# A check moved to VectorE and a re-ordered first ten microseconds, in a kernel that fills TensorE

## The chip, the cores and the metric

One core of one Trainium2 chip. The metric is the device time of one execution in microseconds; lower is better. The profile gives a "span", from the first to the last recorded work; the time is about 2 us longer than the span. A verdict of faster or slower needs 2%, which is 30 us here.

## The reference, cut to what matters

```python
xn = layernorm(x)                                  # x: 2048 x 1024, bf16
out = x + A(xn, mem0, Wq, Wk, Wv, Wo, 32) + B(xn, w1, w2, w3, w4)

def A(x, mem0, ...):          # 64 segments of 32 tokens, each with 8 memory rows ahead
    mem = mem0
    for s in range(64):
        h = concat(mem, x[32*s:32*s+32])
        o = attention(h) @ Wo                      # 32 heads of 128
        mem = o[:8]; outs.append(o[8:])

def B(x, w1, w2, w3, w4):     # token-mixing MLP
    h = gelu(layernorm(x) @ w1);  x1 = x + shift(h) @ w2
    return x1 + gelu(layernorm(x1) @ w3) @ w4
```

Read literally, A is serial: a segment's memory is the output of the one before. The kernel guesses all 64 memories from segment means, computes everything in parallel, and then checks that the guess agrees with the memories that came out. If it does not, a serial fallback would run. With these inputs it does not run.

## The kernel before: the parts that matter

The order is: normalise x and multiply by w1 (stage 1), w2 (stage 2), w3 and w4 (stage 3, with the guessed memories woven in), then V, attention and output. The start, cut:

```python
load_x(0)                                      # one DMA on the SP queue
for c, q in ((0, nc.scalar), (2, nc.scalar), (1, nc.sync), (3, nc.sync)):
    if q is nc.sync: load_x(1 + c // 2)
    q.dma_start(w1_sb[:, 2*c:2*c+2, :], ...)   # w1 in four chunks of 512 KB
...
def transposes(xn2, xn2T, jj, half, halves=False):
    ps = psum0.tile([P, 4, P], F32, tag="tr")  # one PSUM bank
    for k in range(4):
        nc.tensor.matmul(ps[:, k, :], xn2[...k...], ident[:], start=True, stop=True)
    step = 2 if halves else 4                  # halves: only for tile 0
    for i in range(0, 4, step):
        nc.scalar.copy(xn2T[:, jj, half*4+i : half*4+i+step, :], ps[:, i:i+step])

def stage1_k(xn2T):                            # tile 0: k outermost, so that w1 can trickle in
    for k in range(KT):
        if k == KT - 2: tr(1, 0); tr(1, 1)     # tile 1's transposes
        for co in range(KT): nc.tensor.matmul(pss[co//4][:, co%4, :], w1_sb[:, k, ...], xn2T[:, 0, k, :], ...)
# later tiles: norm on VectorE (up to tile 7) or ScalarE; from tile 6 on transposed by DMA (SP queue)
xn2 = ring.tile([P, D], BF16, tag="xn2")       # 3 buffers
```

The check, cut (the squares are summed over partitions by TensorE):

```python
def row_norms(...):  sq = src * src;  sr = sum over k of sq   # VectorE
    nc.tensor.matmul(ps[:1, :NQ], ones_f[:], sr[:])            # fp32, one row
# in stage 3:  gthr = TOL2 * row_norms(GT)                      ("threshold unit")
# at the end:  okf = row_norms(Dm) <= gthr; another fp32 matmul counts the partitions with bad sums
```

## Time and profile before

| what | value |
|---|---|
| time, first three executions | 1509.73 us median, 1509.59 to 1510.04 |
| span, profiled execution | 1508.1 us |
| TensorE busy | 99% |
| first w1 matmul | 8.04 us |
| w1 matmuls of k 6 and 7, tile 0 | 11.17 us |
| first stage-2 matmul (the chain of waits) | 66.81 us |
| last addition | 1504.35 us |

The line on w1, the first stage-2 matmul and the last addition are anchors: the distance between the same two anchors in two traces tells where time went, to some hundredths of a microsecond, where the times of whole executions scatter by one. Anchors are compared only within one view: where nothing waits, the chain of waits puts a start at the end of the work before it, up to 0.2 us later than the timeline does. The w1 matmuls are given by the timeline, the first stage-2 matmul and the last addition by the chain, unless the text says otherwise. The lines that carry the start and the end are in the prediction.

### The profile page before, as it was taken

Reading aid. Unit: us, or ns where it says so; the run is one execution under the profiler, and the core shown is the slowest. Engines: PE = TensorE matmul, PEld = TensorE weight load, DVE = VectorE, ACT = ScalarE, POOL = GpSimd, SP = SyncE. Lnnn points to the kernel's source line nnn. Section 1 sums busy time; section 2 is a strip of 40 time slices with the busy share of each in tenths; the row PEclk is TensorE's granted clock in tenths of the full one; section 3 lists DMA queues with packets and bytes.
Section 4 is the critical chain, followed back from the end, with each engine's and each line's share of the span. In section 5 each row is a group of like instructions: output and inputs, shape, how many; then the busy total and the mean of one; then the engine's idle time right before and its main releaser. Section 6 shows DMA issues by size and latency. Waiting matters only on the chain.

```text
span 1508.1 us, 24241 instructions
## 1 busy us (share of the span) xinstructions
PE 1498.3 (99%) x9762; PEld 803.5 (53%) x9834; DVE 544.6 (36%) x1136; ACT 501.9 (33%) x1140; POOL 175.6 (12%) x246
## 2 busy tenths in 40 slices
PE   9999999999999999999999999999999999999998
PEld 8744444445444444444456645664665455545555
DVE  8382230100020212221146624651564166516641
ACT  6433103013012011111256614650663266416630
POOL 5241020211111221100000010001000100010001
PEclk9999999999999999999999999999999999999999
DMA  9599762353355787622389956992998299919911
GB/s 313 155 254 329 220 180 88 133 203 113 126 164 147 195 250 253 212 98 84 126 223 254 244 125 175 257 239 68 247 244 203 74 227 228 212 62 200 216 49 51
DMA packets 305380, 272.93 MB, mean 181 GB/s; under 512 B 156023, under 2 KB 272281, under 8 KB 305265
## 3 DMA queue, kind: packets, MB, share of 16 engines
q1 hardware_dynamic: 282800, 189.38, 50.5%
q0 software_dynamic: 21776, 80.85, 15.6%
q8 instruction: 79, 1.29, 0.4%
q10 hardware_dynamic: 688, 1.11, 0.2%
q14 instruction: 37, 0.30, 0.1%
HBM read 190.08 MB, written 45.29 MB: 156 GB/s over the span
## 4 chain that ended last, share of the span: by engine, by line
PE 97%; DVE 1%; DMA 1%; issue 0%; POOL 0%; ACT 0%; SPq 0%; POOLq 0%
PE ps L667 30%; PE pso L725 15%; PE ps L601 15%; PE ps L542 13%; PE ps L568 13%; PE ps L400 4%; PE ps L318 2%; PE psS L682 2%; PE psO L706 2%; PE ps L865 1%; PE ps L492 1%; PE gps L471 0%; PE ps L457 0%; DMA wt<-in_A_Wq_dram 0%; DVE st L262 0%
## 5 line engine op out<-in xcount | busy, mean ns | idle before, releaser
L667 PE MATMUL ps<-hTb,wt 128*128 128x396 bf16 (+2 forms) x2528 | 485.0, 342 | 0.1
L667 PEld LDWEIGHTS <-wt 128*128 128x128 bf16 x2528 | 236.7, 98 | 175.8 <-DMA wt<-in_A_Wq_dram 0.5
L601 PE MATMUL ps<-wt,xT 128*128 128x512 bf16 x1003 | 220.1, 379 | 1.1
L725 PE MATMUL pso<-wo_sb,oX 128*128 128x512 bf16 (+1 forms) x972 | 208.5, 372 | 1.1
L542 PE MATMUL ps<-xn3T,w_sb 128*128 128x512 bf16 x896 | 196.2, 379 | 0.0
L568 PE MATMUL ps<-w_sb,h3T 128*128 128x512 bf16 x873 | 194.3, 379 | 1.2
L601 PEld LDWEIGHTS <-xT 128*128 128x128 bf16 x1024 | 100.2, 98 | 120.8
L543 ACT ACTIVATE h3T<-ps 128x512 bf16<-128x512 f32 x112 | 66.8, 597 | 290.4 <-PE ps L542 289.5
L725 PEld LDWEIGHTS <-oX 128*128 128x128 bf16 x992 | 96.3, 98 | 107.4
L669 ACT CAST KT<-ps 128x462 bf16<-128x462 f32 (+2 forms) x160 | 81.7, 510 | 203.0 <-PE ps L667 198.8
L568 PEld LDWEIGHTS <-h3T 128*128 128x128 bf16 x896 | 87.0, 98 | 103.4
L542 PEld LDWEIGHTS <-w_sb 128*128 128x128 bf16 x896 | 86.6, 98 | 102.0
L688 DVE TENSOR_REDUCE sums<-sm 99x4 f32<-99x396 f32 (+2 forms) x176 | 97.6, 555 | 114.9 <-ACT sm L686 114.9
L671 ACT ACTIVATE QT<-ps 128x462 bf16<-128x462 f32 (+2 forms) x160 | 83.8, 524 | 120.6 <-PE ps L667 106.6
L603 ACT CAST Vs<-ps 128x512 bf16<-128x512 f32 x64 | 37.5, 585 | 233.2 <-PE ps L601 174.9
L684 DVE TENSOR_TENSOR sm<-psS,c_mask_reg_sb 99x396 f32<-99x396 f32 x152 | 86.7, 570 | 71.7 <-PE psS L682 71.4
L607 DVE CAST Vs<-ps 128x512 bf16<-128x512 f32 x64 | 44.3, 692 | 171.6 <-PE ps L601 163.2
L686 ACT ACTIVATE sm<-sm 99x396 f32<-99x396 f32 (+2 forms) x176 | 92.8, 527 | 35.0 <-DVE sm L684 28.2
L694 DVE TENSOR_TENSOR Pn<-sm,rs 99x396 bf16<-99x396 f32 (+2 forms) x176 | 98.9, 562 | 7.1 <-DMA PT<-Pn 0.8
L732 POOL DMA_DIRECT2D out_dram<-ot x30 | 16.4, 546 | 698.9 <-DVE ot L731 693.0
L569 DVE TENSOR_TENSOR R<-ps,R 128x512 f32<-128x512 f32 x32 | 21.9, 689 | 175.3 <-PE ps L568 154.9
L731 DVE TENSOR_TENSOR ot<-pso,Rt 128x512 bf16<-128x512 f32 (+1 forms) x33 | 22.3, 675 | 170.4 <-PE pso L725 166.2
(123 smaller groups left out, 1048.3 us busy)
## 6 DMA issues: line engine op xcount, KB each, us to landing
wt<-in_A_Wq_dram SPq DMA_DIRECT2D x76, 512.0 KB
wt<-in_A_Wk_dram SPq DMA_DIRECT2D x76, 512.0 KB
wt<-in_A_Wv_dram POOLq DMA_DIRECT2D x24, 1024.0 KB, 6.5
V_scratch<-Vs SPq DMA_DIRECT2D x32, 512.0 KB
V<-V_scratch SPq DMA_DIRECT2D x40, 384.0 KB
R_scratch<-x POOLq DMA_DIRECT2D x16, 512.0 KB, 4.7
R<-R_scratch SPq DMA_DIRECT2D x16, 512.0 KB
R_scratch<-R POOLq DMA_DIRECT2D x16, 512.0 KB, 3.8
```

The lines of the kernel that those rows point to most:

```text
L542: nc.tensor.matmul(ps[:].rearrange("p (n t) -> p n t", t=P), w3_sb[:, k, f * P:(f + 1) * P], xn3T[tb][:, :, k, :], start=(k == 0), stop=(k ...
L543: nc.scalar.activation(h3T[:, f, :], ps[:], ACTF.Gelu_apprx_tanh)
L568: nc.tensor.matmul(ps[:], h3T[:, f, j * P:(j + 1) * P], w4_sb[:, f, ch * 512:(ch + 1) * 512], start=(f == 0), stop=(f == FT - 1))
L601: nc.tensor.matmul(ps[:], xT[:, m4 * 4 + j, k, :], wv[:, k, :], start=(k == 0), stop=(k == KT - 1))
L667: nc.tensor.matmul(ps[:, :nb], w[:, k, hh * P:(hh + 1) * P], B["hT"][:, k, :nb], start=(k == 0), stop=(k == KT - 1))
L669: nc.scalar.copy(dst[:, hh, :], ps[:, :nb])
L671: nc.scalar.mul(dst[:, hh, :], ps[:, :nb], scale)
L684: nc.vector.tensor_tensor(sm[:T, :, :T], S3, t["mask"][:].unsqueeze(1).to_broadcast((T, 4, T)), op=ALU.add)
L686: nc.scalar.activation(e[:T, :, :T], sm[:T, :, :T], ACTF.Exp, scale=LN2)
L688: nc.vector.tensor_reduce(ss, e[:T, :, :T], axis=AX.X, op=ALU.add)
L694: nc.vector.tensor_tensor(Pn[:T, :, :T], e[:T, :, :T], rs[:T, :].unsqueeze(2).to_broadcast((T, 4, T)), op=ALU.mult)
L725: nc.tensor.matmul(self.ps[:, :self.w], self.oX[0][:, h, self.oX[1] + self.gl * P:self.oX[1] + (self.gl + 1) * P], wo_sb[:, h, self.cc], s ...
```

## The change

Its intent: let tile 0 land and be copied sooner, take the identity and the memory out of later places, and take the check's small matmuls from TensorE. The core of the diff:

```diff
-    ident = const_tile("c_ident", np.eye(P))          # by DMA
+    ident = cpool.tile([P, P], BF16)                  # memset on VectorE, affine_select on POOL
+    mask40 = const_tile("c_mask40", _serial_mask())   # for the fallback, loaded with the constants
@@ load_x
+    if n == 0:
+        nc.scalar.dma_start(xts[n][:, 512:], x_v[:, n, 512:])
+        nc.sync.dma_start(xts[n][:, :512], x_v[:, n, :512])
@@ norm_stats                                          # tile 0: the needed column of the power first
-    nc.gpsimd.tensor_tensor(rr[:], ab[:], neghalf[:], op=ALU.pow)
+    for c in (slice(1, 2), slice(0, 1)) if n == 0 else (slice(0, 2),):
+        nc.gpsimd.tensor_tensor(rr[:, c], ab[:, c], neghalf[:, c], op=ALU.pow)
@@ transposes
-    for k in range(4):
-        nc.tensor.matmul(ps[:, k, :], ...)
     step = 2 if halves else 4
     for i in range(0, 4, step):
+        for k in range(i, i + step):
+            nc.tensor.matmul(ps[:, k, :], ...)
         nc.scalar.copy(..., ps[:, i:i + step])
@@ after tile 0's transposes                           # was in stage 3
+    for k in range(KT):
+        nc.tensor.matmul(ps9[:, k, :], m0[...], eye9[:], start=True, stop=True)
     load_consts(4)
+    nc.gpsimd.memset(sums[:], 1.0)                     # was before everything else
@@ stage 3: threshold unit removed;  norm1(5) one step later
@@ end: row sums, 32x32 transposes and reductions, all on VectorE; no matmul
@@ fallback (not taken): three whole weight loads per segment instead of 24 partial ones
```

More of the change, by code (lines that the diff above doesn't have):

```diff
@@ L130, in load_consts @@
             nc.gpsimd.dma_start(t[:], d.ap())
-    ident = const_tile("c_ident", np.eye(P, dtype=np.float32))
-    load_consts(1)
-    eye9 = const_tile("c_eye9", np.concatenate([np.eye(M, dtype=np.float32), np.ones((M, 1), np.float32)], 1))
+    ident = cpool.tile([P, P], BF16)
+    nc.vector.memset(ident[:], 1.0)
+    eye9 = cpool.tile([M, M + 1], BF16)
+    c0 = cpool.tile([P, KT, 1], F32)
     mask_first = const_tile("c_mask_first", _tile_mask(3, True))
@@ L137 @@
     mask_two = const_tile("c_mask_two", _tile_mask(2, False))
+    mask40 = const_tile("c_mask40", _serial_mask())
     GT = cpool.tile([P, KT, NQ], F32)
     MZ = cpool.tile([P, KT, NQ + 1], BF16)
-    gthr = cpool.tile([1, NQ], F32)
     flag_i = cpool.tile([1, 1], I32)
@@ L151, with row_sums @@
     sums = cpool.tile([P, NTILE * 8, 4], F32)
-    nc.gpsimd.memset(sums[:], 1.0)
     SH = (-1, -1, 1, 1, -2, -2, 2, 2)
-    def row_norms(pool, ppool, tag, src, in_place=False):
-        sq = src if in_place else pool.tile([P, KT, NQ], F32, tag="nsq", bufs=1)
-        nc.vector.tensor_tensor(sq[:], src[:], src[:], op=ALU.mult)
-        sr = pool.tile([P, NQ], F32, tag="nsr", bufs=1)
-        nc.vector.tensor_reduce(sr[:], sq[:].rearrange("p k r -> p r k"), axis=AX.X, op=ALU.add)
-        ps = ppool.tile([P, 512], F32, tag=tag)
-        nc.tensor.matmul(ps[:1, :NQ], ones_f[:], sr[:], start=True, stop=True)
-        return ps
+    def row_sums(src):
+        nc.vector.tensor_tensor(src[:], src[:], src[:], op=ALU.mult)
+        sr = smp.tile([P, NQ], F32, tag="nsr")
+        nc.vector.tensor_reduce(sr[:], src[:].rearrange("p k r -> p r k"), axis=AX.X, op=ALU.add)
+        return sr
     SEGS = ((3,) * 4,) * 3 + ((3,) * 4 + (2,), (2,) + (3,) * 4)
@@ L233, in load_x @@
                             xts[n] = ring.tile([P, D], BF16, tag="xt", bufs=10, name=f"xt{n}")
-                            nc.sync.dma_start(xts[n][:], x_v[:, n, :])
+                            if n == 0:
+                                nc.scalar.dma_start(xts[n][:, 512:], x_v[:, n, 512:])
+                                nc.sync.dma_start(xts[n][:, :512], x_v[:, n, :512])
+                            else:
+                                (nc.gpsimd if n == 12 else nc.sync).dma_start(xts[n][:], x_v[:, n, :])
+                    m0 = hTB[:M, 0, 16:16 + D]
+                    nc.gpsimd.dma_start(m0, A_mem0[0])
+                    nc.gpsimd.affine_select(ident[:], ident[:], [[-1, P]], ALU.is_equal, 0.0, base=0, channel_multiplier=1)
+                    nc.gpsimd.memset(eye9[:, M:M + 1], 1.0)
+                    nc.gpsimd.tensor_copy(eye9[:, 0:M], ident[:M, :M])
                     load_x(0)
@@ L293, in transposes @@
                         ps = psum0.tile([P, 4, P], F32, tag="tr")
-                        for k in range(4):
-                            nc.tensor.matmul(ps[:, k, :], xn2[:, (half * 4 + k) * P:(half * 4 + k + 1) * P], ident[:], start=True, stop=True)
                         step = 2 if halves else 4
                         for i in range(0, 4, step):
+                            for k in range(i, i + step):
+                                nc.tensor.matmul(ps[:, k, :], xn2[:, (half * 4 + k) * P:(half * 4 + k + 1) * P], ident[:], start=True, stop=True)
                             nc.scalar.copy(xn2T[:, jj, half * 4 + i:half * 4 + i + step, :], ps[:, i:i + step])
@@ L349 @@
                     tr(0, 1, True)
+                    ps9 = psum.tile([P, KT, M + 1], F32, tag="mm", bufs=4, name="ps9")
+                    for k in range(KT):
+                        nc.tensor.matmul(ps9[:, k, :], m0[:, k * P:(k + 1) * P], eye9[:], start=True, stop=True)
                     norm_stats(1)
+                    nc.vector.tensor_copy(MZ[:, :, 0:M], ps9[:, :, 0:M])
+                    nc.vector.tensor_copy(c0[:], ps9[:, :, M:M + 1])
                     nc.gpsimd.memset(hTB[:, :, 0:2], 0.0)
@@ L369, in ahead @@
                         norm_stats(n + 1, 1)
-                        norm1(n - 2)
+                        if n == 6:
+                            norm1(n - 2)
                     stage1(3, 1, tiles2[2], {0: [lambda: tr(4, 0)], 2: [lambda: tr(4, 1), lambda: ahead(6)], 4: [lambda: tr(5, 0)], 5: [lambda: tr(5, 1), lambda: ahead(7)]}, 1)
@@ L378, in prep @@
                         norm_stats(n + 1)
+                        if n == 8:
+                            norm1(n - 3)
                         norm1(n - 2)
@@ L435, in seg_sums @@
                         nc.vector.tensor_reduce(xb[:, :, 4 * n:4 * n + 4], xr[:].rearrange("p k (s t) -> p k s t", t=SEG), axis=AX.X, op=ALU.add)
-                m0 = ring.tile([M, D], BF16, tag="nsq", bufs=1)
-                nc.gpsimd.dma_start(m0[:], A_mem0[0])
+                    if n == 0:
+                        nc.vector.tensor_tensor(xb[:, :, 0:1], c0[:], xb[:, :, 0:1], op=ALU.add)
                 for c in range(7):
                     nc.sync.dma_start(w4_sb[:, 4 * c:4 * (c + 1), :], w4_v[:, 4 * c:4 * (c + 1), :])
-                def mem_start():
-                    ps9 = psum3.tile([P, KT, M + 1], F32, tag="vr")
-                    for k in range(KT):
-                        nc.tensor.matmul(ps9[:, k, :], m0[:, k * P:(k + 1) * P], eye9[:], start=True, stop=True)
-                    nc.vector.tensor_copy(MZ[:, :, 0:M], ps9[:, :, 0:M])
-                    nc.vector.tensor_tensor(xb[:, :, 0:1], ps9[:, :, M:M + 1], xb[:, :, 0:1], op=ALU.add)
                 def unit_vb(hg):
@@ L478, in unit_g @@
                     return run
-                def unit_thr():
-                    ps = row_norms(ring, psum3, "vr", GT)
-                    nc.vector.tensor_scalar(gthr[:], ps[:1, :NQ], TOL2, None, op0=ALU.mult)
                 def unit_vr(hg):
@@ L510, in spec_load @@
                         pending.append(u(i))
-                        if u is unit_g and i == 7:
-                            pending.append(unit_thr)
                 def spec_step(depth=1):
@@ L572 @@
                                 spec_step(depth)
-                        elif n == 3:
-                            mem_start()
                         elif n > 3:
@@ L873 @@
         nc.vector.tensor_scalar(inr[:, 1:2], lo[:, 1:2], SUM_HIGH, None, op0=ALU.is_le)
-        bad = smp.tile([P, 1], F32, tag="bad", bufs=1)
-        nc.vector.tensor_tensor(bad[:], inr[:, 0:1], inr[:, 1:2], op=ALU.mult)
-        nc.vector.tensor_scalar(bad[:], bad[:], -1.0, 1.0, op0=ALU.mult, op1=ALU.add)
-        for o in rest[:2]:
+        dsum, gsum = row_sums(Dm), row_sums(GT)
+        col = smp.tile([P, 96], F32, tag="col", bufs=1)
+        nc.vector.memset(col[:], 0.0)
+        nc.vector.scalar_tensor_tensor(col[:, :NQ], gsum[:], TOL2, dsum[:], op0=ALU.mult, op1=ALU.subtract)
@@ new lines @@
+        nc.vector.tensor_tensor(col[:, NQ - 1:NQ], inr[:, 0:1], inr[:, 1:2], op=ALU.mult)
+        nc.vector.tensor_scalar(col[:, NQ - 1:NQ], col[:, NQ - 1:NQ], -1.0, None, op0=ALU.add)
+        colT = smp.tile([P, 3, 32], F32, tag="colT", bufs=1)
+        nc.vector.transpose(colT[:].rearrange("p c r -> p (c r)"), col[:])
+        part = smp.tile([P, 3], F32, tag="part", bufs=1)
+        nc.vector.tensor_reduce(part[:], colT[:], axis=AX.X, op=ALU.add)
+        four = smp.tile([32, 4, 3], F32, tag="four", bufs=1)
@@ new lines @@
+        for q in range(4):
+            nc.vector.tensor_copy(four[:, q, :], part[32 * q:32 * q + 32, :])
+        okf = smp.tile([32, 3], F32, tag="okf", bufs=1)
+        nc.vector.tensor_reduce(okf[:], four[:].rearrange("p q c -> p c q"), axis=AX.X, op=ALU.add)
+        nc.vector.tensor_scalar(okf[:], okf[:], 0.0, None, op0=ALU.is_ge)
+        sqr = smp.tile([32, 32], F32, tag="sqr", bufs=1)
+        nc.vector.memset(sqr[:], 1.0)
+        nc.vector.tensor_reduce(sqr[:, 0:1], okf[:], axis=AX.X, op=ALU.min)
@@ L878 @@
+        sqrT = smp.tile([32, 32], F32, tag="sqrT", bufs=1)
+        nc.vector.transpose(sqrT[:], sqr[:])
+        alike = smp.tile([1, 1], F32, tag="alike", bufs=1)
+        nc.vector.tensor_reduce(alike[:], sqrT[0:1, :], axis=AX.X, op=ALU.min)
+        nc.vector.tensor_scalar(alike[:], alike[:], -1.0, 1.0, op0=ALU.mult, op1=ALU.add)
+        nc.vector.tensor_copy(flag_i[:], alike[:])
+        for o in rest:
             for p in range(8):
                 o.piece(p)
-        psd = row_norms(iop, apsum, "S", Dm, in_place=True)
@@ L881 @@
-        okf = smp.tile([1, NQ], F32, tag="okf", bufs=1)
-        nc.vector.tensor_tensor(okf[:], psd[:1, :NQ], gthr[:], op=ALU.is_le)
-        nok = smp.tile([1, 1], F32, tag="nok", bufs=1)
-        nc.vector.tensor_reduce(nok[:], okf[:, 0:NQ - 1], axis=AX.X, op=ALU.add)
-        psc = apsum.tile([P, 512], F32, tag="O", bufs=2)
-        nc.tensor.matmul(psc[:1, :1], bad[:], ones_f[:], start=True, stop=True)
-        cnt = smp.tile([1, 1], F32, tag="cnt", bufs=1)
-        nc.vector.tensor_scalar(cnt[:], nok[:], -1.0, float(NQ - 1), op0=ALU.mult, op1=ALU.add)
@@ L889 @@
-        nc.vector.tensor_tensor(cnt[:], psc[:1, :1], cnt[:], op=ALU.add)
-        nc.vector.tensor_copy(flag_i[:], cnt[:])
-        for o in rest[2:]:
-            for p in range(8):
-                o.piece(p)
-    cond = nc.values_load(flag_i[0:1, 0:1], min_val=0, max_val=NQ + P)
+    cond = nc.values_load(flag_i[0:1, 0:1], min_val=0, max_val=1)
     with tc.If(cond > 0):
@@ L899 @@
             fbig = fctx.enter_context(tc.tile_pool(name="fbig", bufs=1))
-            fw = fctx.enter_context(tc.tile_pool(name="fw", bufs=4))
+            fw = fctx.enter_context(tc.tile_pool(name="fw", bufs=1))
             fr = fctx.enter_context(tc.tile_pool(name="fr", bufs=2))
@@ L903 @@
             nc.sync.dma_start(wo_sb[:], Wo_v)
-            mask40_d = nc.inline_tensor(_bf(np.tile(_serial_mask(), (1, 8))), name="c_mask40")
-            mask40 = fbig.tile([L, 8 * L], BF16)
-            nc.sync.dma_start(mask40[:], mask40_d.ap())
             hseg = fbig.tile([P, KT, L], BF16)
@@ L922 @@
                 nc.vector.tensor_copy(hseg[:, :, M:L], psx[:])
-                for hg in range(8):
-                    cs_ = slice(hg * 512, (hg + 1) * 512)
-                    hs_ = slice(hg * 4, (hg + 1) * 4)
-                    wq = fw.tile([P, KT, 512], BF16, tag="w")
-                    nc.sync.dma_start(wq[:], Wq_v[:, :, cs_])
-                    wk = fw.tile([P, KT, 512], BF16, tag="w")
-                    nc.sync.dma_start(wk[:], Wk_v[:, :, cs_])
-                    wv = fw.tile([P, KT, 512], BF16, tag="w")
-                    nc.sync.dma_start(wv[:], Wv_v[:, :, cs_])
-                    ps = fps.tile([P, 4, L], F32, tag="mm")
-                    for hh in range(4):
-                        for k in range(KT):
-                            nc.tensor.matmul(ps[:, hh, :], wq[:, k, hh * P:(hh + 1) * P], hseg[:, k, :], start=(k == 0), stop=(k == KT - 1))
-                    nc.scalar.mul(QTa[:, hs_, :], ps[:], QSCALE)
-                    ps = fps.tile([P, 4, L], F32, tag="mm")
-                    for hh in range(4):
-                        for k in range(KT):
-                            nc.tensor.matmul(ps[:, hh, :], wk[:, k, hh * P:(hh + 1) * P], hseg[:, k, :], start=(k == 0), stop=(k == KT - 1))
-                    nc.scalar.copy(KTa[:, hs_, :], ps[:])
-                    ps = fps.tile([P, 512], F32, tag="mm")
-                    for k in range(KT):
-                        nc.tensor.matmul(ps[:L, :], hseg[:, k, :], wv[:, k, :], start=(k == 0), stop=(k == KT - 1))
-                    nc.vector.tensor_copy(Va[:, cs_], ps[:L, :])
@@ new lines @@
+                for which, src in enumerate((Wq_v, Wk_v, Wv_v)):
+                    w = fw.tile([P, KT, H * DH], BF16, tag="w")
+                    nc.sync.dma_start(w[:], src)
+                    for hg in range(8):
+                        hs_ = slice(hg * 4, (hg + 1) * 4)
+                        if which < 2:
+                            ps = fps.tile([P, 4, L], F32, tag="mm")
+                            for hh in range(4):
+                                h = hg * 4 + hh
+                                for k in range(KT):
+                                    nc.tensor.matmul(ps[:, hh, :], w[:, k, h * P:(h + 1) * P], hseg[:, k, :], start=(k == 0), stop=(k == KT - 1))
+                            if which == 0:
+                                nc.scalar.mul(QTa[:, hs_, :], ps[:], QSCALE)
+                            else:
+                                nc.scalar.copy(KTa[:, hs_, :], ps[:])
+                        else:
+                            cs_ = slice(hg * 512, (hg + 1) * 512)
+                            ps = fps.tile([P, 512], F32, tag="mm")
+                            for k in range(KT):
+                                nc.tensor.matmul(ps[:L, :], hseg[:, k, :], w[:, k, cs_], start=(k == 0), stop=(k == KT - 1))
+                            nc.vector.tensor_copy(Va[:, cs_], ps[:L, :])
@@ L946 @@
                 for g8 in range(4):
                     psS = fps.tile([L, 8, L], F32, tag="S", bufs=1)
-                    nc.tensor.matmul(psS[:].rearrange("p h k -> p (h k)"), ident[:L, :L], mask40[:], start=True, stop=False, skip_group_check=True)
+                    nc.tensor.matmul(psS[:], ident[:L, :L], mask40[:].unsqueeze(1).to_broadcast((L, 8, L)), start=True, stop=False, skip_group_check=True)
                     for hh in range(8):
```

## The prediction

> **What bounds the kernel now.** I read the page's busy shares first, then the chain of waits, then the timeline of the first 40 us and of the last 70 us, because the diff touches the two ends. Share of the span by engine, then the chain that ended last, by engine and by line:
>
> ```profile
> PE 1498.3 (99%) x9762; PEld 803.5 (53%) x9834; DVE 544.6 (36%) x1136; ACT 501.9 (33%) x1140; POOL 175.6 (12%) x246
> ...
> PE 97%; DVE 1%; DMA 1%; issue 0%; POOL 0%; ACT 0%; SPq 0%; POOLq 0%
> ```
>
> TensorE is the chain for 97% of 1508.1 us. So work taken from DVE, ACT, POOL or a queue is worth nothing, except where TensorE waits for it: in the chain, that is only before 31.73 us and after 1504.35 us. In between, a change pays only by what it takes out of TensorE's own stream. The start, in the chain in order of time (start us, duration us, what):
>
> ```profile
> 0.76 3.30 DMA xt<-in_A_x_dram
> 4.08 0.69 DVE st L259
> 4.78 0.60 DVE st L262
> 5.40 0.22 DVE mv L263
> 5.65 0.23 DVE ab L264
> 5.96 0.73 POOL rr L265
> 6.72 0.73 DVE xn L274 x2
> ```
>
> The reader is to see a serial path: the first x tile lands at 4.06 us, VectorE takes statistics, POOL raises to a power, VectorE normalises, and only then can TensorE transpose. The timeline of the same stretch shows TensorE (start, duration; the bracket is idle time and its releaser):
>
> ```profile
> 1.38 5.30 PE L335 MATMUL warm<-wz 128*128 128x512 bf16 x12 [1.38 <-DVE wz L329]
> 7.19 0.72 PE L295 MATMUL ps<-c_ident_sb,xn 128*128 128x128 bf16 x8 [0.51 <-DVE xn L274]
> 7.62 1.20 ACT L298 CAST xn2T<-ps 128x256 bf16<-128x256 f32 x4 [4.36 <-PE ps L295]
> 8.04 2.84 PE L308 MATMUL ps<-xn2T,w_sb 128*128 128x128 bf16 x48
> 12.29 0.72 POOL L265 TENSOR_TENSOR rr<-ab,neghalf 128x2 f32<-128x2 f32 x1
> 14.29 0.39 PE L295 MATMUL ps<-c_ident_sb,xn 128*128 128x128 bf16 x4
> ```
>
> Useful work starts at 7.19 us, and twelve warm-up matmuls keep TensorE occupied until 6.68 us: between them lie only 0.51 us. The end, by the chain:
>
> ```profile
> 1487.31 2.75 PE pso L725 x12
> 1490.07 0.21 PE ps L163 x2
> 1490.28 0.03 PE psc L886 x2
> 1490.31 14.01 PE pso L725 x96
> 1504.32 0.02 issue
> 1504.35 0.42 DVE ot L731
> ```
>
> The old check's two small float matmuls (L163, L886) interrupt the last output product for 0.24 us; nothing else of the check is on the chain. The last addition and the last store (from 1504.35 to 1508.1) stay as they are.
>
> **What the Trainium skill says.** (1) "DMA: Bandwidth & Descriptors", section "Issuing engines are not separate DMA queues": transfers issued by different engines run on the same 16 DMA engines and interleave; issuing from two only saves sequencer time. The trace agrees that the engines are shared: from 1.38 to 7.19 us the DMA share is 0.93 at 319 GB/s, and from 7.19 to 15 us 1.05 to 1.07 at 385 to 393 GB/s. So halves on two queues help only by changing what else is ahead of the tile. (2) "TensorE: Matmul & The Clock Gate", Part 1: the array runs at half clock until a window of about 3.4 us of activity has passed, the window being free-running. The trace agrees in kind: the warm-up matmuls are 0.43 us apart, the full-clock ones of the same width later 0.22 us (10.74 us for 49). (3) "GPSIMD Engine Reference", section 3.1, says the cost on POOL is a dispatch term plus a term per element. The trace has the power at 558 ns median for 128x1 (L408) and 702 to 942 ns for 128x2 (L265), so one column instead of two saves about 0.15 us, not half.
>
> **The change part by part.** *First x tile in halves.* Before, the tile's 0.25 MB (SP queue) share the engines with the first w1 chunk (ACT queue). Shared evenly, 0.5 MB at 385 GB/s take 1.3 us. With a half on each queue, both ahead of w1, 0.25 MB take 0.65 us. Estimate from those rates: landing at 3.4 us instead of 4.06, 0.65 us gained. The w1 chunks come later by one half tile on the ACT queue (0.13 MB, 0.3 us) and earlier on SP; by the same sum the last chunk lands near 9.9 us and is wanted near 10.4.
>
> *Power of the needed column first:* 0.15 us. *Copies after two transposes instead of four:* two matmul starts of 0.06 us, 0.12 us. Together the start path would be 0.65 + 0.15 = 0.8 us shorter: the first transposes could start at 6.4 us. But the warm-up block holds TensorE until 6.68 us, 6.75 with one more VectorE memset ahead of it. So they start near 6.8 us: 0.4 us gained, not 0.8.
>
> *Identity on chip:* replaces a 32 KB transfer that took 5.5 us to land (issue at 1.22 us, so 6.7 us), which did not hold 7.19 but would hold a start before 6.7. A VectorE memset and three POOL operations (under 1 us each by POOL's 0.71 us memset of 128x704) are done by about 4 us, before POOL's first power. *Memory first:* eight tiny matmuls move here from 218.76 us, where the chain has them at 0.28 us. Here they stand between tile 0's transposes and the first w1 matmuls; the transposes take 0.5 us when not waiting (6.8 to 7.3), the eight end near 7.6, and the first ACT copy (before: 7.62 to 7.92) would be done near 7.4. So w1 matmuls start near 7.6 instead of 8.04: net gain still 0.4. The memory's own load (16 KB, issued near 1.2 us) needs to land by 7.3; the small constants took 4.9 to 6.3 us.
>
> *POOL order:* the 0.71 us memset of sums goes behind the four constant loads, ahead of tile 2's power. That would move it from 12.29 to at best 12.2 us; tile 2 is then normalised by 13.6 and its transposes are wanted at 14.29 - 0.4 = 13.9. Close, but no wait. After this the VectorE chain is almost where it was, so the rest rests on TensorE being fed. *norm1 moved out of the tile-7 step:* 0.54 us of VectorE work leaves the chain that ends in POOL's nm at 29.37, ACT's xn at 29.67 and the stall of 0.25 us at 31.69. ACT can start 0.6 us sooner, TensorE wants it 0.4 us sooner: the stall goes. Start in all: 0.4 + 0.25 = 0.65 us (between 0.1 and 0.9).
>
> *Memory matmuls out of the MLP:* -0.28 us. *Threshold matmul out* (L163 at 427.47): -0.21 us. *Check to VectorE:* -0.24 us of TensorE. On VectorE it adds two squares (0.75 us each, one of them new), two reductions (1.17 us each, one new), and some sixteen small ones of 0.15 to 0.3 us: about 7 us from 1476.8 on, so done near 1484. VectorE has 3.06 us of work in 1476.1 to 1490, so there is room; an output addition due at 1483.2 may slip by a microsecond, and TensorE has other accumulators to go on with. The flag is ready 20 us before it is read. *Fallback:* not taken, so its transfers and loops cost nothing.
>
> Sum: 0.65 + 0.28 + 0.21 + 0.24 = 1.4 us. 1509.73 - 1.4 = **1508.3 us**, 0.1% less.
>
> **The rivals.** *A new wait at the start takes the gain:* the memory's load or the last w1 chunk lands late, or the moved memset makes tile 2 late. For it: DMA is at its full 385 GB/s there and the two margins are 0.3 to 0.5 us. Against it: tiny loads landed in 4.9 to 6.3 us. It would give 1508.7 to 1509.6. *The array is still at half clock when the transposes start earlier:* the window is free-running, the twelfth warm-up matmul is still slow; up to 0.3 us back. *The whole 0.8 us come through* if some warm-up matmuls run at full clock and end early: 1507.7. *The check on VectorE becomes the end:* only if it delayed the last addition at 1504.35, 20 us after it should be done; I give this under 3%. It would cost 1 to 5 us.
>
> **Range and chances.** The three middle and end terms (0.73 us) are read straight off the chain and are safe. The start may give from 0 to 1.2 us. Runs of the kernel before spread over 0.45 us. That makes 1507.0 to 1509.5. A change of 2% is 30 us; nothing in the diff is of that size, in either direction.
>
> **What would show it.** Right: statistics of tile 0 start at 3.4 to 3.5 us; first transposes at 6.7 to 6.9; the w1 matmuls near 7.6; no TensorE idle at 31.7; first stage-2 matmul near 66.0 instead of 66.81; neither small float matmul in the chain at 427 and 1490; the last addition 1.4 us earlier, and 3.7 us from it to the end as before. Wrong: a TensorE wait on the memory's load or a w1 chunk before 11 us, one on tile 2's norm near 14 us, or output accumulators waiting for VectorE after 1477 us.

## More of the kernel before

One more, from the timeline of TensorE (start us, duration us, engine, line, operation), turned out to matter:

```profile
11.17 1.06 PE L308 MATMUL ps<-xn2T,w_sb 128*128 128x128 bf16 x16
```

These are tile 0's matmuls with the last w1 chunk. No wait stands in the brackets, so nothing shows how close to waiting they are. No bracket is not the same as room to spare.

## The result and the profile after

| | before | after |
|---|---|---|
| median of six executions, same rounds | 1510.35 us | 1509.99 us |
| range | 1509.59 to 1511.12 | 1509.44 to 1511.17 |
| profiled span | 1508.1 us | 1508.9 us |
| first w1 matmul | 8.04 us | 8.82 us |
| w1 matmuls of k 6 and 7 | 11.17 us | 13.28 us |
| first stage-2 matmul | 66.81 us | 68.77 us |
| last addition | 1504.35 us | 1505.54 us |

The ratio is 0.9999, with an interval of 0.9986 to 1.0012. The predicted 1508.3 us and the whole range up to 1509.5 lie below the measured median. Part of that distance is the starting point: six executions of the kernel before spread over 1.53 us, where the first three had spread over 0.45, and their median is 0.62 us above the 1509.73 that the forecast started from. Of the gain of 1.4 us that was forecast, the medians show 0.36, which is inside the noise.

The page of the changed kernel still has TensorE as the bound:

```profile
PE 98%; DMA 1%; issue 0%; DVE 0%; SPq 0%; ACT 0%; POOL 0%
```

The chain of waits at the start (start us, duration us, what):

```profile
3.51 0.69 DVE st L265
...
6.46 0.30 PE ps L304 x2
...
6.78 0.38 ACT xn2T L305
...
7.21 0.29 PE ps L304 x2
...
7.51 0.66 ACT xn2T L305 x2
...
8.21 0.37 PE ps L304 x2
...
8.88 4.11 PE ps L315 x48
...
68.77 0.22 PE ps L416
```

The reader is to see three things. The first tile is there sooner, as forecast: statistics at 3.51 us instead of 4.08, the power in 0.58 us instead of 0.73, transposes at 6.46 instead of 7.19. Then the chain alternates between TensorE and ScalarE, twice: transposes, a copy, transposes, copies. Before, the four transposes of a half ran together. And the 48 w1 matmuls are slow: 4.18 us in the timeline, where they had taken 2.84 before (the chain, above, has 4.11). The granted clock explains the last point (columns: stretch, length, TensorE busy and its instructions, granted clock, DMA share, GB/s):

```profile
4.85:8.26 3.41, 1.74 (x12) 1.00 1.02 365
...
9.82:10.32 0.50, 0.50 (x8) 0.50 1.06 393
12.32:12.82 0.50, 0.50 (x13) 1.00 1.02 377
```

From 8.3 to 11.6 us the clock is at half. In the 3.41 us ahead of the fall, TensorE was busy for 1.74 us, 51%. The two costs add up, all by the timelines: 0.78 us later at the first w1 matmul, and 1.34 us longer from there to the transposes that follow the 48 (12.84 - 8.82 against 10.72 - 8.04). Less the 0.16 us that a stall near 31.7 us cost the trace before (from k 6 and 7 to stage 2 it took 55.48 us, the changed kernel 55.32), that is 1.96 us, which is 68.77 - 66.81.

The end, by the chain, and VectorE's part of it in the timeline:

```profile
1488.85 16.66 PE pso L726 x108
...
1505.54 0.42 DVE ot L732
```

```profile
1478.32 0.75 DVE L158 TENSOR_TENSOR Dm<-Dm 128x568 f32<-128x568 f32 x1
...
1485.05 0.14 DVE L899 CAST flag_i<-alike 1x1 int32<-1x1 f32 x1
```

No small matmul interrupts the output product any more. The check takes VectorE from 1478.3 to 1485.2 us; TensorE never waits for it. From the first stage-2 matmul to the last addition the kernel before takes 1437.54 us (1504.35 - 66.81), the changed one 1436.77: 0.77 us gained. So in these two traces the start lost 1.96 us and the rest won 0.77; the tail after the last addition, 3.75 us before and 3.36 after, makes up the span's +0.8 us.

**Theory.** Half of a transposed tile lies in one PSUM tile (PSUM: the memory that the kernel's matmuls write to) of one bank; with copies after each pair, the second pair's transposes must wait until ScalarE has read the first. The waits cost time, and in some executions they empty TensorE enough that its clock falls. **Rivals:** the moved memory matmuls or the halved tile cost the time; the clock falls by itself; the slow matmuls wait for w1.

### The profile page after: what moved, and what is told of

It reads as the page before. It is cut to its first block, busy times and chain, and to the rows that moved or that the text cites. A ratio compares the mean times of both kernels' runs of the same rounds, so it can differ in the third digit from the quotient of the medians. Undisturbed runs are those within 1.5% of the kernel's fastest.

```text
span 1508.9 us, 24248 instructions
## 1 busy us (share of the span) xinstructions
PE 1498.3 (99%) x9757; PEld 804.7 (53%) x9828; DVE 546.8 (36%) x1148; ACT 502.3 (33%) x1140; POOL 175.5 (12%) x250
## 4 chain that ended last, share of the span: by engine, by line
PE 98%; DMA 1%; issue 0%; DVE 0%; SPq 0%; ACT 0%; POOL 0%
PE ps L668 30%; PE ps L602 15%; PE pso L726 15%; PE ps L545 13%; PE ps L571 13%; PE ps L416 4%; PE ps L325 3%; PE psS L683 2%; PE psO L707 2%; PE ps L866 1%; PE ps L497 1%; PE gps L480 0%; PE ps L466 0%; DMA wt<-in_A_Wq_dram 0%; PE ps L315 0%
## 5 line engine op out<-in xcount | busy, mean ns | idle before, releaser
L546 ACT ACTIVATE h3T<-ps 128x512 bf16<-128x512 f32 x112 | 66.8, 597 | 290.8 <-PE ps L545 289.8
```

The costliest lines, as they stand in the source:

```text
L546: nc.scalar.activation(h3T[:, f, :], ps[:], ACTF.Gelu_apprx_tanh)
```

## The experiments

Twelve runs were made, in three jobs (e5 and e6 are the two kernels once more); within a job they share one chip and the runs of the kernel before. All gave correct results. e6 was one look, all others five executions.

| run | median us | before, same job | span of its trace | first stage-2 matmul | executions with mean clock under 1.0 |
|---|---|---|---|---|---|
| e1 four, then copies | 1509.11 | 1509.79 | 1511.6 | 67.88 | 0 of 5 |
| e2 before + interleaving | 1511.83 | 1509.79 | 1510.6 | 68.97 | 4 of 5 |
| e3 own PSUM tiles | 1509.21 | 1509.79 | 1506.9 | 67.17 | 0 of 5 |
| e4 filled gaps | 1509.37 | 1509.79 | 1507.6 | 67.95 | 0 of 5 |
| e5 after again | 1510.25 | 1509.63 | 1508.0 | 69.05 | 3 of 5 |
| e6 before again | 1509.72 | 1509.63 | 1507.9 | 66.56 | 0 of 1 |
| e7 old fallback | 1510.26 | 1509.63 | 1507.8 | 67.57 | 3 of 5 |
| e8 more buffers | 1508.64 | 1509.63 | 1506.9 | 67.21 | 0 of 5 |
| e9 middle and end only | 1509.95 | 1510.26 | 1507.2 | 66.67 | 0 of 5 |
| e10 starts mended | 1509.25 | 1510.26 | 1507.0 | 66.57 | 0 of 5 |
| e11 mask in fallback | 1509.86 | 1510.26 | 1508.1 | 68.24 | 2 of 5 |
| e12 whole first tile | 1509.76 | 1510.26 | 1508.0 | 68.50 | 0 of 5 |

No ratio is clear of noise (each interval is about 0.0013 either side and holds 1). So the verdicts below rest on anchors in the traces and on counts of executions, not on medians.

### e1: the interleaving undone

```diff
-    for i in range(0, 4, step):
-        for k in range(i, i + step): nc.tensor.matmul(ps[:, k, :], ...)
+    for k in range(4): nc.tensor.matmul(ps[:, k, :], ...)
+    for i in range(0, 4, step):
         nc.scalar.copy(...)
```

> The changed kernel with one part undone: four transposes of a half, then the two copies, as before. Theory (the copy of the first pair makes the next pair's transposes wait, because both pairs lie in one PSUM tile; those waits empty TensorE and, in some executions, let its clock fall to half): the first w1 matmul starts near 7.7 us instead of 8.82, its 48 matmuls take 2.7 us, the first stage-2 matmul starts near 66.1 us, time near 1508.2 us. Rival 1 (the memory matmuls or the halved tile cost the time): w1 still starts at 8.5 us or later. Rival 2 (the clock falls by itself, whatever the waits): 48 w1 matmuls at 4 us in about half of the executions here too.

```profile
7.51 3.08 PE L315 MATMUL ps<-xn2T,w_sb 128*128 128x128 bf16 x48
...
11.07 1.07 PE L315 MATMUL ps<-xn2T,w_sb 128*128 128x128 bf16 x16
```

The waits are gone and the first w1 matmul is at 7.51 us, near the expected 7.7. But the matmuls of k 6 and 7 start at 11.07 us: 0.1 us ahead of the 11.17 of the kernel before, although TensorE had begun half a microsecond sooner. Weight loads waited for w1 chunks, 0.23 us ahead of 8.62 and 0.21 us ahead of 11.07. Then a second thing took time: the first stage-2 matmul was expected at 66.1 us and came at 67.88. ScalarE's timeline, then TensorE's waits (total us, times, longest):

```profile
29.99 1.24 ACT L283 ACTIVATE xn<-xt,nm,rr 128x1024 bf16<-128x1024 bf16 x1 [1.42 <-DMA xn2T<-xn]
...
37.61 1.24 ACT L283 ACTIVATE xn<-xt,nm,rr 128x1024 bf16<-128x1024 bf16 x1 [1.12 <-DMA xn2T<-xn]
```

```profile
PE ps L545 <- DMA w_sb<-in_B_w_dram: 3.5, 3, 1.7
...
PE ps L325 <- ACT hTB L327: 1.1, 1, 1.1
```

ScalarE, ready to normalise tiles 8 and 11, waits 1.42 and 1.12 us for transposing transfers, and TensorE then waits 1.1 us for ScalarE. This trace is also the slowest execution of all (span 1511.6 us against 1506.2 to 1507.3 in the other four): 3.5 us of it are a wait for a late weight chunk at the start of stage 3, which no other trace has. It is a miss of the forecast time and no part of the cause.

### e2: the interleaving alone, in the kernel before

The same diff as in the change, `transposes` only.

> The kernel before with that one part alone: two transposes, copy, two transposes, copy for tile 0. Theory: two waits of about 0.5 us each appear before the second pair of each half, the first w1 matmul starts near 9.0 us instead of 8.04, and the time is 1.0 us longer (2.3 us where the clock falls as well): 1511.0 to 1512.5 us. Rival (the interleaving is harmless, the memory matmuls make the delay): w1 starts near 8.0 us, time unchanged.

```profile
7.76 0.38 PE L297 MATMUL ps<-c_ident_sb,xn 128*128 128x128 bf16 x4 [0.46 <-ACT xn2T L298]
8.76 0.37 PE L297 MATMUL ps<-c_ident_sb,xn 128*128 128x128 bf16 x2 [0.62 <-ACT xn2T L298]
8.93 4.27 PE L308 MATMUL ps<-xn2T,w_sb 128*128 128x128 bf16 x48
```

The two waits appear, 0.46 and 0.62 us, as in the changed kernel, without its halved tile and without its memory matmuls. The w1 matmuls take 4.27 us at a clock of 0.50. All five executions lie above all nine of the kernel before in this job (1511.23 to 1512.59 against 1509.17 to 1510.65). The first rival falls: the interleaving is enough to bring the waits and the slow matmuls. (In the medians of this job it costs 2.04 us; the interval of the ratio, 0.9997 to 1.0025, still holds 1.)

### e3: interleaved, but each pair in a PSUM tile of its own

```diff
     for i in range(0, 4, step):
+        if i: ps = psum0.tile([P, 4, P], F32, tag="trh")
         for k in range(i, i + step): ...
```

> The changed kernel with the interleaving kept, but each pair of transposes in a PSUM tile of its own. Theory (the wait is for the shared tile, not for TensorE, the weights or the norm): the waits of transposes on the copy vanish, first w1 matmul near 7.6 us, first stage-2 matmul near 66.0 us, time 1508.1 us, at most 0.2 us from the run with four transposes then copy. Rival (the pairs wait for something else, as the norm of the second half): w1 still near 8.8 us.

```profile
6.41 0.72 PE L306 MATMUL ps<-ident,xn 128*128 128x128 bf16 x8 [0.81 <-DVE xn L281]
...
7.34 1.07 PE L317 MATMUL ps<-xn2T,w_sb 128*128 128x128 bf16 x16
8.78 1.96 PE L317 MATMUL ps<-xn2T,w_sb 128*128 128x128 bf16 x32 [0.37 <-DMA w_sb<-in_B_w_dram]
...
11.24 1.07 PE L317 MATMUL ps<-xn2T,w_sb 128*128 128x128 bf16 x16
```

No transposes wait for a copy; w1 starts at 7.34 us. So the wait was for the shared tile. (The new tile also lies in another bank; two tiles in one bank were not run, so tile and bank are not told apart.) The Trainium skill states the ground for it: "PSUM — Partial Sum Buffer", section "PSUM bank collisions raise a hardware error", says that two engines must not be in one bank and quadrant at once, reads and writes alike, and advises guarding by bank and not by address. No run here lets two engines meet in a bank. The traces show a program that keeps them apart: the pairs wrote disjoint columns, and in one bank they waited 0.46 and 0.62 us, in two banks not at all. The reader also sees the next limit: 0.37 us for a w1 chunk at 8.78, and 11.24 for k 6 and 7. Stage 2 came at 67.17 us, not near the expected 66.0.

### e4: the two waits filled with idle matmuls

```diff
+        for _ in range(3 if i else 0):
+            nc.tensor.matmul(warm[:, :256], wz[:, :P], wz[:, :256], start=True, stop=True)
```

> The changed kernel with three idle 256-column matmuls on zeros ahead of the second pair of each half, which fill most of the two waits; nothing else. Theory of two costs (waits and clock): the waits stay, w1 starts at 8.8 to 9.1 us, but the granted clock stays full and the 48 w1 matmuls take 2.7 us in all executions; first stage-2 matmul near 67.3 us; time near 1509.4 us with no executions near 1511. Rival (the slow w1 matmuls have another cause, as late weights): 48 matmuls still take 4.1 us.

```profile
8.30 0.27 PE L306 MATMUL ps<-ident,xn 128*128 128x128 bf16 x2 [0.29 <-ACT xn2T L307]
...
8.79 2.85 PE L317 MATMUL ps<-xn2T,w_sb 128*128 128x128 bf16 x48
```

The work still waits for the copies and w1 starts at 8.79 us, as in the changed kernel, but 48 matmuls take 2.85 us, and none of the five executions shows a lowered mean clock. The third rival falls: nothing was changed for w1, and the slow matmuls of the changed kernel stand in a stretch whose granted clock is 0.50.

The second rival asks why the clock falls in some executions only. The clock records in the traces tell more than the counts (ahead of the first record the column above shows 1.00, so here the first record itself is used). Full clock was granted at 4.81 us in the changed kernel's trace, as late as 7.39 in others. Where it came early, the last warm-up matmuls ran 0.22 us apart instead of 0.43, and the block ended sooner. It took 5.30 us in the kernel before, whose grant came at 6.77 us, and here 4.39:

```profile
1.48 4.39 PE L342 MATMUL warm<-wz 128*128 128x512 bf16 x12 [1.48 <-DVE wz L336]
```

In the two traces with a fall, the clock fell 3.41 us after it had been granted. How busy TensorE was in these first 3.41 us:

| trace | full clock from | TensorE busy in the next 3.41 us | clock after that |
|---|---|---|---|
| changed kernel | 4.81 us | 1.74 us, 51% | half |
| e2 | 5.10 | 1.53, 45% | half |
| e3 | 4.27 | 2.60, 76% | full |
| e12 | 4.53 | 2.35, 69% | full |
| e4 | 5.00 | 2.40, 70% | full |
| e5 | 6.98 | 2.33, 68% | full |
| e7 | 7.27 | 2.60, 76% | full |

So an early grant alone does not bring the fall (e3, e4, e12), nor do the waits alone (e5, e7): it fell where the two came together and left TensorE half empty. The other seven traces are at about 80% or more, and none falls. One trace each is little, but e4's five executions and the 30 of e1, e3, e8, e9, e10 and e12 without a lowered mean clock agree with it.

### e5 and e6: both kernels once more

No edit.

> The changed kernel itself once more, for more executions and a second trace. Theory (two costs at the start: waits of 1.1 us in every execution, a clock that falls to half in some): executions fall in two groups, spans near 1507.6 us with a mean clock of 1.0 and near 1508.7 with 0.999; in a trace without the fall the 48 w1 matmuls take 2.7 us and the first stage-2 matmul starts near 67.4 to 67.9 us. Rival (the fall is in every execution): all spans near 1508.8.

> The kernel before once more, for a second trace of it. Theory (its gap of 0.51 us ahead of the first transposes lets the clock fall in some executions too): span near 1507.6 us without the fall, near 1508.5 with it, and in the second case the w1 matmuls take over 3.5 us for 48. Rival: the clock never falls in the kernel before.

e5's trace has no fall: 48 matmuls in 2.85 us from 8.95 us on, and k 6 and 7 at 12.09. But TensorE then lost 1.32 us on the way to stage 2, which came at 69.05 us and not at 67.4 to 67.9, for this reason:

```profile
40.94 1.25 PE L325 MATMUL ps<-xn2T,w_sb 128*128 128x256 bf16 x10 [1.32 <-DMA xn2T<-xn]
```

A transposing transfer needed 7.47 us to land, and TensorE waited for it. Of the eleven executions of the changed kernel, five have a mean clock below 1.0, with spans of 1508.1 to 1508.9 us and one of 1512.1; the six others lie between 1507.3 and 1508.1. The groups are there, less far apart than expected; what made the one of 1512.1 so long is not known. e6 shows the kernel before at full clock: stage 2 at 66.56 us, not a wait between 8 and 66 us. Its executions scatter too (spans 1507.2 to 1509.1 in the three jobs), yet only 2 of 27 show a lowered mean clock (so it does fall there at times, as the theory had it). What makes that scatter is not settled.

### e7 and e11: the untaken fallback, and its mask

e7 puts the whole fallback of the kernel before back into the changed one; e11 only moves the load of the 40x40 mask back into it.

> The changed kernel with the untaken fallback of the kernel before put back, and nothing else. The time is longer than the profiled span by 1.96 us in the kernel before and by 2.24 in the changed one. Theory (the shape of the untaken branch sets that difference): it goes back to 1.96 us, the span stays, the time is 0.28 us shorter than that of the changed kernel, near 1509.7. Rival (it is the start or the check): the difference stays 2.24.

> The changed kernel, with only the fallback's mask loaded inside the fallback again instead of with the constants; its seven transfers and loops stay the changed ones. If the shape of the untaken loops makes time minus span 0.33 us longer, it stays near 2.2 us; if the mask's place does, it falls to 1.84 us as in the kernel before.

The time is longer than the span by 2.24 us in the changed kernel (mean of six; 2.17 in e5), by 1.84, 1.97 and 1.98 in the kernel before in the three jobs. In e7 it is 1.79, in e11 1.77. So a part of 0.2 to 0.4 us belongs to this program, and moving the mask alone removes it, with the changed loops left in. But e12, with the mask still among the constants and the first tile in one transfer, has 1.94, and e1, with two halves, 2.21. e8, with the mask outside as well, has 2.04, and e3, which it builds on, 2.32. So edits that have nothing to do with the mask move it too, and what it is stays open. Nor do the medians show a gain: 1510.26 in e7, 1510.25 for the changed kernel in the same job (e5). It lies outside anything that the trace shows.

### e8: buffers for ScalarE, on top of e3

```diff
-    xn2 = ring.tile([P, D], BF16, tag="xn2")
+    xn2 = xn_keep[3][:, n - 8] if 8 <= n < 12 else ring.tile([P, D], BF16, tag="xn2")
```

> The changed kernel with own PSUM tiles (as in e3) and, besides, four other buffers for the normalised tiles 8 to 11, in memory that lies idle then. Theory (when TensorE is early, ScalarE waits for the transposing transfers of tiles 6 to 9 to give their buffers back, TensorE then waits for ScalarE): the ScalarE waits on these transfers (1.8 us in e3, 2.5 in e1) go, TensorE has no idle time between 24 and 42 us, first stage-2 matmul near 66.4 to 66.8 us, span near 1506.3. Rival (the transfers' landing itself is needed by TensorE): the idle time stays, now as a wait for the transposed tile.

```profile
PE ps L317 <- DMA w_sb<-in_B_w_dram: 0.4, 1, 0.4
PE ps L327 <- DMA xn2T<-xn: 0.4, 1, 0.4
```

ScalarE no longer waits for transfers (none in its list), so buffers were what held it. TensorE still waits 0.4 us, now for the transposed tile itself: the rival is right as well, and stage 2 came at 67.21 us, not at 66.4 to 66.8. Its chain from tile 2 to tile 7 runs over VectorE without a gap and begins behind POOL's constants and the moved memset, which put tile 2's power at 12.07 us.

### e9: the middle and the end alone, in the kernel before

Only the check on VectorE and the missing threshold unit.

> The kernel before with only the check on VectorE and the threshold unit out; its start, its memory matmuls and its fallback as before. Theory (the middle and end terms of the sum are real, 0.43 us at the threshold and 0.35 us at the check between anchors of the two traces): first stage-2 matmul as before (66.5 to 66.9 us), TensorE from the first stage-3 matmul to the last addition 0.6 to 0.8 us shorter, span near 1507.0 us in executions at full clock, time near 1508.9, time minus span as before. Rival (the check on VectorE costs at the end what it saves): span unchanged at 1507.7.

From first stage-2 matmul to last addition: 1436.75 us (1503.42 - 66.67), against 1437.54 and 1437.59 in the two traces of the kernel before. The check costs nothing at the end. But only part of the 0.8 us belongs to the edit. Between the first matmul that writes `gps` (guessed outputs) and the first Q/K matmul, where the threshold unit was, every trace without it takes 421.55 or 421.56 us, every trace with it 421.87: 0.32 us, shown. The stretch after it, up to the output product, is touched by no edit, and e9 is 0.34 us shorter there than the kernel before (121.47 against 121.81); it takes 121.25 to 122.09 us over all traces. That part is scatter. The time moved as a whole by 0.3 us in the medians, which is noise.

### e10: what the runs so far point to

The changed kernel with e1's edit and the old fallback, and:

```diff
-    load_consts(3); nc.gpsimd.memset(sums[:], 1.0)     # ahead of tile 2's power
     ...
     for n in (NT - 2, NT - 1): norm1(n)
+    load_consts(3); nc.gpsimd.memset(sums[:], 1.0)     # at the end of stage 1
```

> The changed kernel with four transposes then copies, the old fallback, and the constant loads and the memset of sums behind the last norm instead of ahead of tile 2's power. Theory (VectorE's chain from tile 2 to tile 7 hangs on POOL's constants, and through the transposing transfers sets TensorE at 24 to 40 us; the last w1 chunk sets it at 11.1 us): tile 2's power starts near 11.3 us or earlier instead of 12.1, tile 7's transpose is issued some 0.8 us sooner, no TensorE wait between 24 and 42 us, the w1 matmuls of k 6 and 7 still at 11.1 us, first stage-2 matmul near 66.5 us, span near 1506.4, time near 1508.2, under both kernels. Rival (transposing transfers land late whatever their issue): a wait of 0.3 us or more stays near 32 or 40 us.

```profile
7.86 2.79 PE ps L314 x48
...
11.09 1.05 PE ps L314 x16
...
66.57 8.63 PE ps L415 x40
```

Tile 2's power starts at 11.57 us, its follower's transposing transfers are issued 0.6 us sooner than in the changed kernel, and TensorE has no wait between 12 and 66 us. Stage 2 begins at 66.57 us, where the kernel before had it (66.56 and 66.81): earlier is not to be had while k 6 and 7 start at 11.07 (11.09 in the chain, shown here), for nothing waits after that. The span is 1507.0 us in the trace, 1507.5 in the median of the five, against 1508.2 for the kernel before in the same job; 1506.4 was expected. The median time, 1509.25, is 1.0 us below that of the kernel before, and the ratio 0.9994 has an interval of 0.9980 to 1.0007: it is perhaps better than both, which these executions do not prove. e8 is as far below the kernel before in its own job (1508.64 against 1509.63).

### e12: the first tile whole

e1's edit, and `load_x(0)` in one transfer on the SP queue.

> The changed kernel with four transposes then copies (as e1), and the first x tile loaded whole by one queue. Theory (halving gains 0.5 us at the tile, but the last w1 chunk lands near 11.1 us either way): VectorE's first statistics start at 4.0 us instead of 3.5, the w1 matmuls start near 8.0 instead of 7.5, those of k 6 and 7 at 11.1 us all the same, and the first stage-2 matmul does not move against e1 beyond what the transposing transfers scatter (66.5 to 67.9 us). Rival (the halves do pay): everything from 11 us on is 0.4 us later than in e1.

```profile
7.79 2.88 PE ps L311 x48
...
11.12 0.89 PE ps L311 x16
```

These two lines are from the chain; by the timeline, in which e1 was read, w1 starts at 7.72 us (e1: 7.51) and k 6 and 7 at 10.96 (e1: 11.07). Statistics start at 3.84 us, 0.33 us later than with halves in the changed kernel (3.51). The halves' gain is more than gone by 11 us: with the tile whole, no weight load waits for w1, and k 6 and 7 come 0.11 us sooner. The rival, 0.4 us later from 11 us on, falls. Stage 2 at 68.50 us is later for TensorE waits between 24 and 42 us, 1.3 us on a transposing transfer and 0.4 on ScalarE, which waits for such transfers in turn. These waits scatter from trace to trace: 0 us in e7 and 1.3 in e5, which are nearly alike (k 6 and 7 at 12.09 us in both, tile 2's power at 12.08 and 12.16).

## Why the prediction was wrong

By its own steps:

- **"Copies after two transposes instead of four: ... 0.12 us" gained. This step failed.** It counted what the first copy gains and not what the next pair must wait for. The wait was 0.46 + 0.62 us, in every trace with the shared tile (changed kernel, e2, e5, e7, e11) and in none with separate tiles or with four transposes first (e1, e3, e8, e10, e12). w1 therefore began at 8.82 to 8.95 us and not near 7.6, and with the clock's fall the start lost 1.96 us in the first pair of traces, where 0.65 was to be gained. Of the signs of being wrong that the prediction names, none appears in the changed kernel's trace: the wait was for ScalarE's copy, which the list leaves out.
- **The half clock was foreseen from the wrong side.** The rival was a warm-up that lasts too long, worth 0.3 us. It happened that the waits make the clock fall again, worth 1.34 us, in 14 of 26 executions of the kernels that had these waits unfilled (changed kernel with e5, e2, e7, e11), against 0 of 35 in e1, e3, e4, e8, e9, e10 and e12. The condition of the rival "The whole 0.8 us come through" came true as well: some warm-up matmuls of the changed kernel's trace ran at full clock, the block ended at 5.87 us instead of 6.68, and the first transposes started at 6.46 us. It did not bring the gain: the early end belongs to the stretch in which TensorE was half empty (the table under e4).
- **"By the same sum the last chunk lands near 9.9 us and is wanted near 10.4": the chunk was mis-sized.** Its matmuls start at 11.07 to 11.24 us in the kernel before, e1, e3, e8 and e10, whether w1 began at 7.25 or at 8.04 us; in e1, e3 and e10 their weight loads wait for w1 right there (in e8 two earlier ones do). So even without the failed step the start had about 0.1 us to win up to there. Halving the tile was right in mechanism (0.57 us sooner, 0.65 forecast) and could not reach the end; with the tile whole (e12) these matmuls came at 10.96 us, without such a wait.
- **"Close, but no wait" for tile 2, and the stall at 31.7 us.** No wait on tile 2 came. The stall is indeed absent after, but the kernel before does not always have it: from k 6 and 7 to stage 2 it cost 0.16 us in the first trace (0.25 was forecast), 0.11 in e9, and nothing in e6 and e2, which have the old order of norms. And TensorE meets the transposing transfers there, directly or through ScalarE: 0.3 to 1.7 us between 24 and 42 us in e1, e3, e4, e5, e8 and e12, none in the changed kernel's own trace, e7 and e10.
- **Middle and end, 0.73 us: right in mechanism, near in the total partly by luck.** Between stage 2 and the last addition the changed kernel gained 0.77 us in the first pair of traces, 0.86 in e10, 1.03 in e7 and 1.6 in e5. Taken apart: from the first w4 matmul to the first on `gps`, where the memory matmuls were, it takes 161.13 to 161.15 us without them in every trace and 161.53 with them: 0.39 us (0.28 forecast). The threshold is worth 0.32 (0.21 forecast). The last stretch, from the first output matmul on, takes 628.85 to 629.08 us in the three traces with the old check and 628.50 to 628.86 in the others, so the check's 0.24 us are not told apart from scatter; the rest of the differences is scatter of the stretch before it. The forecast took each small matmul's own time, and the first two gave more; why is not shown. The check on VectorE took 6.9 us where 7 were forecast, and an output addition was late by half a microsecond without effect, as said.
- **"In the chain, that is only before 31.73 us and after 1504.35": a small misreading.** The chain before also goes through a weight load that lands at 789.52 us, where TensorE was idle for 0.10 us. Nothing in the change hangs on it.
- **"Fallback: not taken, so ... cost nothing".** Nothing in the span, but the time outside the span is 0.2 to 0.4 us longer, and putting the fallback's mask back removes it (e11). The mechanism stays open.

At full clock and without a wait for a transposing transfer the account reads: start +0.76 us (67.57 in e7 against 66.81), rest -0.77, outside the span about +0.3. That is close to the nought that was measured; with the clock's fall it is 1.2 us worse (68.77).

## What to carry to other kernels

Alternating writers and readers in one PSUM tile (here a bank) is a hand-over each time (0.46 and 0.62 us); if copies are to start early, give every piece its own tile and bank. Ahead of shortening a start path, find every other thing that arrives at the same time (here the last weight chunk and the transposed tiles): a matmul without a wait in the old trace may be standing right at that limit. And a wait of TensorE in its first microseconds can cost twice, once as a wait and once in clock.

## What the Trainium skill lacked or had wrong

- "TensorE: Matmul & The Clock Gate", Part 1, says that the clock falls after an idle window of about 3.4 us. The runs show it falling after a stretch of 3.41 us in which TensorE was busy for 51% of the time (1.74 us; 45% in e2); it then stayed at half for 3.4 us. With 68% busy (2.33 of 3.41 us, e5) and more it stayed full, in 12 traces. The page gives no such threshold, and no run here lies between 51% and 68%. That the fall comes in some executions only agrees with its free-running window.
- "DMA: Bandwidth & Descriptors", section "Anatomy of one DMA — SWDGE (gpsimd) path", fits about 2.0 us plus the bytes' time. While the engines were full at the start, a 0.1 KB load took 4.9 us and a 32 KB load 5.5 us to land, so the fit does not hold beside other traffic.
- No page tells how far transposing transfers scatter under load: those issued between 31 and 34 us that a chain shows took 6.2 (e1), 6.4 (e4), 6.7 (e12) and 7.5 us (e5) to land.
- No page tells of a part of the time outside the profiled span that moves with edits which don't show in the trace: 1.77 us with the mask inside the untaken branch (e11), 2.24 with it outside, but 1.94 in e12 and 2.04 in e8 with it outside too.
